# Splitting four of the stores by rows: the last one, and three of the side stores, in a decode layer with its backward pass

## The chip, the cores and the metric

The kernel runs on one core of a Trainium2 chip. The core has TensorE (matmul and transpose), VectorE, ScalarE and GpSimd for computing, SyncE (SP), which here only issues transfers, and sixteen DMA engines that carry data between HBM and the on-chip memory (SBUF, 128 partitions). The metric is the device time of one execution in microseconds, lower is better.

## The reference, cut to what matters

One decode step (batch 4, one new token, width 512) of a pre-norm transformer layer with a cached attention (32 heads, 4096 cached positions, head size 128) and a gated feed-forward part of width 1792, forward and backward:

```python
def _A_ref(x, k_cache, v_cache, wq, wo):
    q = (x @ wq).reshape(B, Sq, H, Dh).transpose(0, 2, 1, 3)
    scores = jnp.einsum("bhqd,bhkd->bhqk", q, k_cache) * (Dh ** -0.5)
    p = _softmax(scores, axis=-1)
    o = jnp.einsum("bhqk,bhkd->bhqd", p, v_cache)
    return o.transpose(0, 2, 1, 3).reshape(B, Sq, H * Dh) @ wo
def _B_ref(x, w1, w3, w2):
    h = _silu(x @ w1) * (x @ w3)
    return h @ w2
h = x + _A_ref(_layernorm(x), k_cache, v_cache, wq, wo)
out = h + _B_ref(_layernorm(h), w1, w3, w2)
```

The outputs are `out` and its vector-Jacobian products with a given `grad_out`, in bfloat16: for x (`out_1`), for k_cache (`out_2`), for v_cache (`out_3`), for wq (`out_4`), wo (`out_5`), w1 (`out_6`), w3 (`out_7`) and w2 (`out_8`). There is one query position only, so the gradient of each of the 128 heads' K is the outer product of a column of 4096 numbers and a row of 128 (likewise for V). The two cache gradients are by far the largest outputs: 4 x 32 x 4096 x 128 numbers each, 134 MB. The gradient of each weight is an outer product too, summed over the 4 rows of the batch.

## The kernel before, in words

All large data lives in one SBUF tensor, `arena`, cut into 23 slots of 4160 numbers a partition (`Slot`). Two neighbouring slots together are a `Slot2`. A slot is taken from a list of free ones, filled, used, and given back; who takes it next waits for the transfer that last read or wrote it. The order of the work of every engine is the order of the program text: the schedule is manual.

Forward. Heads are read one after the other, K and V, a slot each (1024 KB: 128 partitions of 8 KB). VectorE and TensorE transpose K, TensorE makes the scores, and a small matrix is kept for each head for the gradient of q. Then comes the feed-forward part with its gradients for h.

Backward. V is read a second time. The first 32 heads are done one at a time (`front`, `group_dS`, `grad_K`, `grad_V`), the other 96 heads in 48 pairs: a pair fills a `Slot2`, 128 partitions of 16 KB, 2048 KB. In the loop over pairs (`for t in range(NT)`), in this order: V pairs are loaded ahead (`load_pairs`, L1319); `front_pair` transposes a pair of V (TensorE L795, ScalarE L796) and multiplies it with the incoming gradient (L1351); `more_V` makes pairs of the gradient of V (`grad_pair` to `out_3`); `grad_pair` to `out_2` makes the pair's gradient of K. `grad_pair` takes a `Slot2`, lets VectorE write the outer product (`outer_pair`, L1422) and stores it with one transfer on SP's queue (L1432). GpSimd prepares the columns for these products (`P2_pair`, L1419) and the windows for `front_pair` (`dO_pair`, L1331). The very last of these stores, that of `out_2` for pair 47, is the last transfer of the program.

Between these, `side(s)` advances the generator `side_work` by a step or two. It makes the small gradients: x and wq, then w2 (two stores of 128 rows of 7 KB, L1174), w1 and w3 (four stores, L1190), and wo (four stores of 128 rows of 8 KB, L1201). Each piece of 512 columns is one matmul (`grad_unit`), copied out of the accumulator by ScalarE (L1030) one piece later (`grad_flush`). When a slot is full, its store is issued on SP's queue, in 128 rows, one a partition.

All transfers but a few tiny ones go through SP's queue, in program order. SP uses eight semaphores for them in turn, so a transfer is issued only when the eighth before it has landed. GpSimd's own queue carries the few tiny ones (for instance the four rows of `oflat`, L1179).

Of the kernel before, what the change touches and what calls it, by code (L numbers as in the profile page):

```python
# [29 lines left out]
def kernel(  # L30
# [22 lines left out]
    nc = tc.nc  # L53
    P = nc.NUM_PARTITIONS

    B = A_x.shape[0]
    D = A_x.shape[-1]
    H = A_k_cache.shape[1]
    Sk = A_k_cache.shape[2]
    Dh = A_k_cache.shape[3]  # L60
# [6 lines left out]
    SJ = Sk // P  # L67
# [138 lines left out]
    for i in range(2):  # L206
        t = fcon.tile([P, 64], BF16, name=f"onesw{i}")
# [4 lines left out]
    def ones_window(col):  # L212
# [11 lines left out]
                          in_=rowg[:, None, :, None].to_broadcast([P, 4, 8, 4]))  # L224
# [635 lines left out]
    with ExitStack() as cm:  # L860
# [72 lines left out]
        for fc in range(FC):  # L933
            c = fc % 2
# [82 lines left out]
    with ExitStack() as c2:  # L1017
# [9 lines left out]
        def grad_flush():  # L1027
            if gu:
                dst, ps, n = gu.pop()
                nc.scalar.copy(out=dst, in_=ps[:, 0:n])  # L1030


        def grad_unit(dst, lhsT, rhs):
            n = rhs.shape[-1]
            ps = psg.tile([P, 512], FP32, tag="gps", name="gps")
            nc.tensor.matmul(ps[:, 0:n], lhsT=lhsT, rhs=rhs, start=True, stop=True)
            grad_flush()
            gu.append((dst, ps, n))
# [33 lines left out]
        def side_work():  # L1072
# [10 lines left out]
            t = rs.f(2048)[:, 1536:1536 + NH]  # L1083
# [49 lines left out]
            for cc in range(DC):  # L1133
                st = Slot("gwq")
# [32 lines left out]
            for i in range(2):  # L1167
                st = Slot("gw2")
                hw = hh_rows[:, i * 7 * P:(i + 1) * 7 * P].rearrange("b (p k) -> b k p", k=7)
                for k in range(7):  # L1170
                    grad_unit(st.b(7 * D)[:, k * D:(k + 1) * D], hw[:, k, :], gr_bf)
                    yield
                grad_flush()
                nc.sync.dma_start(out=out_8[i * 7 * P:(i + 1) * 7 * P, :].rearrange("(p c) j -> p c j", c=7),  # L1174
                                  in_=st.b(7 * D).rearrange("p (c j) -> p c j", c=7))
                st.give()
            oflat = Slot("oflat")
            for b in range(B):
# [1 line left out]
            for (rows, out_ap) in ((dg_rows, out_6), (du_rows, out_7)):  # L1180
                for i in range(2):
                    st = Slot("gw13")
                    nw = hhat_bf[0:B, i * 2 * P:(i + 1) * 2 * P].rearrange("b (p k) -> b k p", k=2)
                    for k in range(2):
                        for (f0_, w_) in f_chunks:
# [5 lines left out]
                                      in_=st.b(2 * F).rearrange("p (c f) -> p c f", c=2))  # L1191
                    st.give()
            r1.give()
            for h0 in range(0, H, 8):
                st = Slot("gwo")
                ow = oflat.b(HD)[0:B, h0 * P:(h0 + 8) * P].rearrange("b (p k) -> b k p", k=8)
                for k in range(8):
                    grad_unit(st.b(8 * D)[:, k * D:(k + 1) * D], ow[:, k, :], dh_bf)
                    yield
                grad_flush()  # L1200
                nc.sync.dma_start(out=out_5[h0 * P:(h0 + 8) * P, :].rearrange("(p k) j -> p k j", k=8),  # L1201
                                  in_=st.b(8 * D).rearrange("p (k j) -> p k j", k=8))
                st.give()
            oflat.give()
            r2.give()
            part["side_done"] = True

        units["s"] = side_work()


# [91 lines left out]
        NT = (NH - SP) // 2  # L1302
# [8 lines left out]
        def two_heads(ap, t):  # L1311
            b, h = t % B, H0 + t // B * 2
            return ap[b, h:h + 2].rearrange("h (p j) d -> (h p) (j d)", p=P // 2)
# [107 lines left out]
        def outer_pair(dst, col2, row):  # L1421
            nc.vector.tensor_tensor(  # L1422
                out=dst.rearrange("p (j r t) -> p j r t", r=Dh // 2, t=2),
                in0=col2[:, :, None, :].to_broadcast([P, 2 * SJ, Dh // 2, 2]),
                in1=row.rearrange("p (r t) -> p r t", t=2)[:, None, :, :].to_broadcast([P, 2 * SJ, Dh // 2, 2]),
                op=ALU.mult,
            )

        def grad_pair(out_ap, t, col2, row):
            g_ = Slot2()  # L1430
            outer_pair(g_.t[:, 0:2 * SJ * Dh], col2, row)
            nc.sync.dma_start(out=two_heads(out_ap, t), in_=g_.t[:, 0:2 * SJ * Dh])  # L1432
            g_.give()

        O0, S0, S1, L, LP = 2, 21, 35, 5, 3
# [2 lines left out]
        def more_V(upto):  # L1438
            while gvd["n"] < min(SP, upto):
                s = gvd["n"]  # L1440
                P_group(s // B)
                replicate("rdo", s - s % REP)
                grad_V(s)
                P_group(s // B + 1)
                gvd["n"] += 1
                if s % REP == 2 and 2 < s < SP - 2:
                    replicate("rdo", s + 2)
                elif s == SP - 2:
                    replicate_pair("rdo", 0)
                if s >= SP - 2:  # L1450
                    P2_pair(s - SP + 2)
            while gvd["t"] < NT and SP + 2 * gvd["t"] + 2 <= upto:
                t = gvd["t"]
                P2_pair(t)
                replicate_pair("rdo", t // B)
                grad_pair(out_3, t, pP2.pop(t), reps["rdo", "p", t // B][:, t % B, :])
                P2_pair(t + 1)
                gvd["t"] += 1
                if t % B == 2:
                    replicate_pair("rdo", t // B + 1)  # L1460
# [57 lines left out]
        for t in range(NT):  # L1518
            s = SP + 2 * t
            load_pairs(t + LP)  # L1520
            if t % B == 2:
                replicate_pair("rq", t // B + 1)
            if t + LP < NT:
                front_pair(t + LP, lambda: side(s))
            else:
                if t + LP == NT:
                    rows_out()
                    rows_T()
                side(s)
            more_V(s + 2 + lead_V(s))  # L1530
            grad_pair(out_2, t, pdS[t // 2][:, t % 2], reps["rq", "p", t // B][:, t % B, :])
            if t % 2 == 1 and t + 1 < NT:
                group_dS_pair((t + 1) // 2)
            side(s + 1)
# [31 lines left out]
```

## Time and profile before

| | |
|---|---|
| time, median of 3 runs | 1681.93 us (1681.45 to 1684.35) |
| the profiled execution's own time | 1680.53 us |
| its span, first to last instruction | 1678.7 us |
| moved by DMA | 705.31 MB, mean 420 GB/s |
| HBM read / written | 420.75 MB / 282.34 MB |
| TensorE / VectorE / ScalarE / GpSimd busy | 75% / 71% / 58% / 23% |
| a 2048 KB store, issue to landing (median) | 27.3 us |
| issue of an SP transfer (L1432, median) | 0.33 us |

Times in the views are microseconds from the start of the span. The page cuts the span into 40 equal slices; the digits after an engine's name are its busy share in tenths, those after DMA the mean busy share of the sixteen DMA engines. "Issue to landing" is the time until the last of the sixteen engines' shares has arrived; the trace records all sixteen landings of each transfer, but not by the engines' numbers. A window's line gives the stretch, its length, busy time and number of instructions of each computing engine, the granted TensorE clock, the DMA share and GB/s. DMA shares come from whole packets, so in short windows they are coarse, and a full load can read 1.01 or 1.02. A line of waits says who waited for whom: total us, times, longest.

### The profile page before, as it was taken

Reading aid. Unit: us, or ns where it says so; the run is one execution under the profiler, and the core shown is the slowest. Engines: PE = TensorE matmul, PEld = TensorE weight load, DVE = VectorE, ACT = ScalarE, POOL = GpSimd, SP = SyncE. Lnnn points to the kernel's source line nnn. Section 1 sums busy time; section 2 is a strip of 40 time slices with the busy share of each in tenths; the row PEclk is TensorE's granted clock in tenths of the full one; section 3 lists DMA queues with packets and bytes.
Section 4 is the critical chain, followed back from the end, with each engine's and each line's share of the span. In section 5 each row is a group of like instructions: output and inputs, shape, how many; then the busy total and the mean of one; then the engine's idle time right before and its main releaser. Section 6 shows DMA issues by size and latency. Waiting matters only on the chain.

```text
span 1678.7 us, 33156 instructions
## 1 busy us (share of the span) xinstructions
PE 1264.2 (75%) x13899; PEld 884.7 (53%) x13899; DVE 1194.9 (71%) x1000; ACT 969.8 (58%) x1545; POOL 381.1 (23%) x665
## 2 busy tenths in 40 slices
PE   5999889889888889877777657667667777767650
PEld 4777777777677776643433334444444444444330
DVE  5888888888888887667766558586566566555683
ACT  3555545555555554677667557567666676666650
POOL 1221223222232223333313313211111112101020
PEclk9999999999999999899999888886666676666775
DMA  9999999999999999999999999999999999999996
GB/s 402 419 425 424 425 425 425 425 423 424 415 417 407 424 403 411 405 407 426 426 427 428 429 430 430 430 430 429 430 430 430 429 429 432 429 431 430 429 430 285
DMA packets 82229, 705.31 MB, mean 420 GB/s; under 512 B 8716, under 2 KB 14744, under 8 KB 16544
## 3 DMA queue, kind: packets, MB, share of 16 engines
q1 hardware_dynamic: 81664, 703.10, 99.3%
q8 instruction: 109, 1.79, 0.4%
q14 instruction: 40, 0.33, 0.0%
q0 software_dynamic: 416, 0.10, 0.0%
HBM read 420.75 MB, written 282.34 MB: 419 GB/s over the span
## 4 chain that ended last, share of the span: by engine, by line
DMA 74%; DVE 10%; PE 8%; ACT 3%; issue 2%; DVEq 0%; POOL 0%; SPq 0%; ACTq 0%
DMA out_dram<-arena 38%; DMA arena<-in_A_k_cache_dram 27%; DMA arena<-in_A_v_cache_dram 7%; DVE arena L1422 7%; PE M_ps L468 2%; ACT arena L796 2%; PE pt_tps L355 1%; DVE arena L830 1%; DVE arena L454 1%; DMA arena<-arena 1%; ACT Pn L433 1%; DMA arena<-in_A_wq_dram 1%; PE pt_tps L795 1%; DMA arena<-in_A_wo_dram 1%; PE b_ps L411 1%
## 5 line engine op out<-in xcount | busy, mean ns | idle before, releaser
L796 ACT COPY arena<-pt_tps 128x1024 bf16<-128x1024 bf16 x512 | 491.1, 1026 | 243.7 <-PE pt_tps L795 240.4
L795 PE MATMUL pt_tps<-ident_f,arena 128*128 128x128 f32 x2048 | 400.7, 348 | 200.8 <-DMA arena<-in_A_v_cache_dram 116.2
L795 PEld LDWEIGHTS pt_tps<-ident_f,arena 128*128 128x128 f32 x2048 | 292.9, 176 | 371.0 <-issue 189.3
L1422 DVE TENSOR_TENSOR arena<-arena 128x8192 bf16<-128x8192 bf16 x48 | 212.4, 4426 | 203.4 <-DMA out_dram<-arena 183.8
L454 DVE TENSOR_TENSOR arena<-arena 128x4096 bf16<-128x4096 bf16 x128 | 289.9, 2265 | 4.9 <-POOL arena L450 4.6
L468 PE MATMUL M_ps<-arena 128*128 128x130 bf16 x4096 | 282.4, 221 | 4.5 <-DMA arena<-in_A_v_cache_dram 4.3
L468 PEld LDWEIGHTS <-arena 128*128 128x128 bf16 x4096 | 252.8, 99 | 20.9 <-DMA arena<-in_A_v_cache_dram 11.1
L1422 DVE TENSOR_TENSOR arena<-dS,arena 128x8192 bf16<-128x8192 bf16 x48 | 212.4, 4427 | 54.9 <-DMA out_dram<-arena 54.9
L361 DVE STREAM_TRANSPOSE arena<-arena 128x512 f32<-128x512 f32 (+1 forms) x258 | 239.9, 947 | 0.0
L356 ACT COPY arena<-pt_tps 128x1024 bf16<-128x1024 bf16 x128 | 127.8, 1013 | 183.8 <-PE pt_tps L355 183.5
L1419 POOL COPY arena<-arena 128x128 bf16<-128x128 bf16 x48 | 48.2, 1005 | 385.2 <-DVE arena L1422 266.7
L367 POOL TENSOR_TENSOR W<-qrep,wmask 128x128 bf16<-128x128 bf16 x128 | 113.9, 890 | 82.8 <-PE S_ps L387 68.2
L450 POOL COPY arena<-P_all 128x64 bf16<-128x64 bf16 x128 | 31.0, 242 | 402.9 <-ACT P_all L444 296.8
L1331 POOL COPY arena<-arena 64x4 bf16<-64x4 bf16 x96 | 80.9, 843 | 135.6 <-PE dP_ps L1351 114.2
L355 PE MATMUL pt_tps<-ident_b,arena 128*128 128x128 bf16 x1024 | 79.7, 224 | 37.8 <-DMA arena<-in_A_k_cache_dram 37.6
L830 DVE TENSOR_TENSOR arena<-dS,arena 128x4096 bf16<-128x4096 bf16 x32 | 73.5, 2299 | 36.4 <-DMA out_dram<-arena 35.9
L433 ACT ACTIVATE Pn<-E,rl 128x1024 bf16<-128x1024 f32 x64 | 73.5, 1149 | 36.4 <-DVE rl L430 36.1
L1351 PE MATMUL dP_ps<-arena 128*32 128x512 bf16 x768 | 85.2, 479 | 7.0 <-ACT arena L796 6.8
L355 PEld LDWEIGHTS <-arena 128*128 128x128 bf16 x1024 | 62.5, 100 | 48.0 <-DMA arena<-in_A_k_cache_dram 47.0
L387 PE MATMUL S_ps<-arena,W 128*32 128x256 bf16 x1536 | 81.3, 285 | 0.5 <-DVE arena L361 0.2
L444 ACT COPY P_all<-pt_P 32x64 bf16<-32x64 bf16 x256 | 51.9, 203 | 48.6 <-PE pt_P L440 46.4
L478 PE MATMUL kP_ps<-arena,onesw 128*32 128x512 bf16 x1024 | 79.2, 386 | 0.0
(257 smaller groups left out, 1363.9 us busy)
## 6 DMA issues: line engine op xcount, KB each, us to landing
out_dram<-arena SPq DMA_DIRECT2D x96, 2048.0 KB, 27.3
arena<-in_A_v_cache_dram SPq DMA_DIRECT2D x160, 1024.0 KB, 16.2
arena<-in_A_k_cache_dram SPq DMA_DIRECT2D x128, 1024.0 KB, 17.9
arena<-in_A_v_cache_dram SPq DMA_DIRECT2D x48, 2048.0 KB, 31.7
out_dram<-arena SPq DMA_DIRECT2D x72, 1024.0 KB, 19.9
arena<-in_A_wq_dram SPq DMA_DIRECT2D x8, 1024.0 KB, 17.0
arena<-in_B_w_dram SPq DMA_DIRECT2D x6, 896.0 KB, 11.8
out_dram<-arena SPq DMA_DIRECT2D x6, 896.0 KB, 26.1
```

Of the source, the lines that this page charges most:

```text
L355: nc.tensor.transpose(pt[:, i, :], Kn[:, c * GW + i, :], ident_b[:])
L356: nc.scalar.copy(out=KT[:, c * GW:(c + 1) * GW, :], in_=pt[:])
L361: nc.vector.transpose(out=KT[:, c * w_:(c + n) * w_], in_=Kn[:, c * w_:(c + n) * w_])
L367: nc.gpsimd.tensor_tensor(out=W[:, hl], in0=qrep[:, :, s:s + 1].to_broadcast([P, 4, 32]), in1=wmask[:, hl, None, :].to_broadcast([P, 4, 32 ...
L433: nc.scalar.activation(out=st["Pn"][:], in_=st["E"][:, :, None, :].to_broadcast([P, JQ, 4, 32]), func=AF.Copy, scale=rl[:])
L454: nc.vector.tensor_tensor(out=PK[:, :, 0:Dh].rearrange("p j (r t) -> p j r t", t=2), in0=Ks[s].heads().rearrange("p j (r t) -> p j r t", t=2),
L468: nc.tensor.matmul(hold["M"][:], lhsT=Vn[:, j, :], rhs=PK[:, j, :], start=(j == 0), stop=(j == SJ - 1))
L795: nc.tensor.transpose(ptw[:, jj, :], w[:, 4 * g + jj, :], ident_f[:])
L796: nc.scalar.copy(out=v.rearrange("p (j d) -> p j d", d=Dh)[:, g * GW:(g + 1) * GW, :], in_=pt[:])
L830: nc.vector.tensor_tensor(out=dst.rearrange("p j (r t) -> p j r t", t=2), in0=col2[:, :, None, :].to_broadcast([P, SJ, Dh // 2, 2]), in1=r ...
L1351: nc.tensor.matmul(rows["acc"][32 * c:32 * (c + 1), :], lhsT=zt[t % B][:, k, ZP - m:ZP - m + 32], rhs=words_of(v, 2 * c + u, k), start=(pl ...
L1422: nc.vector.tensor_tensor(out=dst.rearrange("p (j r t) -> p j r t", r=Dh // 2, t=2), in0=col2[:, :, None, :].to_broadcast([P, 2 * SJ, Dh / ...
```

## The change

Four stores are cut by rows (partitions); the bytes, the source and the destination stay the same.

- The last store of all (`out_2`, pair 47, 128 rows of 16 KB) becomes two transfers on SP's queue: first rows 92 to 127 (36 rows), then rows 0 to 91 (92 rows, which run on four DMA engines).
- The two stores of the gradient of w2 (`out_8`, 128 rows of 7 KB) become three transfers each on SP's queue: 112, 11 and 5 rows for the first, 112, 10 and 6 rows for the second.
- The first of the four stores of the gradient of wo (`out_5`, 128 rows of 8 KB) becomes 112 rows on SP's queue and two parts, of 7 and of 9 rows, on GpSimd's queue.

```diff
@@ side_work, gradient of w2 @@
-                nc.sync.dma_start(out=out_8[i * 7 * P:(i + 1) * 7 * P, :].rearrange("(p c) j -> p c j", c=7),
-                                  in_=st.b(7 * D).rearrange("p (c j) -> p c j", c=7))
+                cuts = ((0, 112), (112, 123), (123, P)) if i == 0 else ((0, 112), (112, 122), (122, P))
+                for (p0, p1) in cuts:
+                    nc.sync.dma_start(out=out_8[i * 7 * P:(i + 1) * 7 * P, :].rearrange("(p c) j -> p c j", c=7)[p0:p1],
+                                      in_=st.b(7 * D).rearrange("p (c j) -> p c j", c=7)[p0:p1])
                 st.give()
@@ side_work, gradient of wo @@
-                nc.sync.dma_start(out=out_5[h0 * P:(h0 + 8) * P, :].rearrange("(p k) j -> p k j", k=8),
-                                  in_=st.b(8 * D).rearrange("p (k j) -> p k j", k=8))
+                for (eng, p0, p1) in ((nc.sync, 0, 112), (nc.gpsimd, 112, 119), (nc.gpsimd, 119, P)) if h0 == 0 else ((nc.sync, 0, P),):
+                    eng.dma_start(out=out_5[h0 * P:(h0 + 8) * P, :].rearrange("(p k) j -> p k j", k=8)[p0:p1],
+                                  in_=st.b(8 * D).rearrange("p (k j) -> p k j", k=8)[p0:p1])
                 st.give()
@@ grad_pair @@
-            nc.sync.dma_start(out=two_heads(out_ap, t), in_=g_.t[:, 0:2 * SJ * Dh])
+            last = out_ap is out_2 and t == NT - 1
+            for (p0, p1) in ((92, P), (0, 92)) if last else ((0, P),):
+                nc.sync.dma_start(out=two_heads(out_ap, t)[p0:p1], in_=g_.t[p0:p1, 0:2 * SJ * Dh])
             g_.give()
```

The order of the computing engines' instructions stays as it was. SP issues five transfers more, GpSimd two.

## The prediction

> **What bounds the kernel now.** I read the page first, for what the whole span is limited by.
>
> ```profile
> span 1678.7 us, 33156 instructions
> DMA  9999999999999999999999999999999999999996
> GB/s 402 419 425 424 425 425 425 425 423 424 415 417 407 424 403 411 405 407 426 426 427 428 429 430 430 430 430 429 430 430 430 429 429 432 429 431 430 429 430 285
> q1 hardware_dynamic: 81664, 703.10, 99.3%
> DMA 74%; DVE 10%; PE 8%; ACT 3%; issue 2%; DVEq 0%; POOL 0%; SPq 0%; ACTq 0%
> ```
>
> All sixteen DMA engines are busy in every slice but the last, and from the middle on they move 430 GB/s without a dip. TensorE, VectorE and ScalarE have room. So no compute instruction is worth anything here, and only two things are: fewer bytes (the change moves the same bytes) and the way the engines finish. The last slice stands at six tenths. I therefore looked at the DMA view of the last 39 us alone, in slices of 0.975 us, and at windows over the same stretch (the last two columns are DMA share and GB/s).
>
> ```profile
> DMA  9897999989999899999997755520000000000000
> GB/s 437 370 504 336 504 437 387 487 370 471 437 387 504 353 471 437 387 504 387 437 420 303 336 235 252 235 118 34 34 17 34 17 34 34 17 34 17 34 0 0
> ```
> ```profile
> 1650.00:1660.00 10.00, 0.00 (x0) 0.00 (x0) 1.85 (x1) 0.00 (x0) 0.00 (x0) 0.50 1.02 437
> 1664.00:1665.00 1.00, 0.00 (x0) 0.00 (x0) 0.00 (x0) 0.00 (x0) 0.00 (x0) 0.50 0.57 246
> 1667.00:1677.00 10.00, 0.00 (x0) 0.00 (x0) 0.00 (x0) 0.00 (x0) 0.00 (x0) 0.50 0.07 28
> ```
>
> Until 1660 the share is 1: sixteen engines. At 1664 it is 0.57, about nine. From 1667 to 1677 it is 0.07, and 1/16 is 0.0625: for ten microseconds one engine alone works off its part of the last stores at 28 GB/s, about what each of sixteen has at 430 GB/s (26.9). The kernel's end is this one engine. The trace's landing records, sixteen for each transfer, say it exactly. The last store's sixteen shares landed at 1660.74, then 1661.24, 1661.25, 1661.30 and 1661.43, then nothing until 1663.41 and 1663.88, then eight between 1665.51 and 1666.91, and the last at 1677.82; the span ends 0.9 later. The late engine is not an accident of the end: its landing behind the median one is 1.7 us for a store issued at 731, 3.8 at 913, 5.7 at 1095, 8.7 at 1299, 10.8 at 1483, 12.3 for the last.
>
> Third, the issue side, for what stands behind the last store.
>
> ```profile
> SPq L1432 <- DVE arena L1422: 567.7, 93, 13.8
> 1643.21 9.00 SPq L1432 DMA_DIRECT2D out_dram<-arena  x3
> DMA to landing us min/median/max: 15.4/27.3/31.8
> ```
>
> The last store is issued at 1651.88 and lands 25.9 us later, behind what its engines have queued. SP mostly waits for VectorE, so another issue of 0.33 us (median of that line) is hidden.
>
> **The change part by part.** The sum is made against the profiled execution: span 1678.7, own time 1680.53, so 1.83 outside the span. The median of the three runs, 1681.93, is 1.4 above it; I carry the difference over to the median.
>
> *A row.* A 2048 KB store is 128 rows of 16 KB, eight an engine. At 430 GB/s it takes 2.097 MB / 430 = 4.88 us, 0.61 us a row; the late engine's last landings are 4.83 to 4.87 apart, 0.607 a row, which I use. The tail shows that an engine working alone keeps that rate. Rows of 7 KB and 8 KB are taken in proportion, 0.267 and 0.305.
>
> *Last store.* Before, eight rows on each engine. After, 92 rows on four engines, 23 each, and 36 rows. That 92 go on four I read as the largest equal division over at most sixteen (92 = 4 x 23); then 36 go on twelve, 3 each, and I assume both counts start from the same end of the row of engines. The four then have 26 rows (18 more, +10.93 us), the next eight have 3 (5 fewer, -3.04), the remaining four none (8 fewer, -4.86). [...]
>
> *Side stores* (L1174 twice, L1201 once). By the same division 112 rows give 7 an engine, and 11 + 5 (then 10 + 6) put one row each on the first eleven and five (ten and six). The first four gain one row of 7 KB in each, +0.53; the last four lose one in each, -0.53. Of the out_5 store, 16 of 128 rows go as 7 + 9 through GpSimd: any engine loses one 8 KB row and gets zero to two, so -0.31 to +0.31; I take 0, as sixteen rows over sixteen engines.
>
> *Issues.* Five more on SP, each 0.33 us: hidden by the 567.7 us above. Two on GpSimd, 0.54 us each (median of the four at L1179), at about 1493 behind the wait for ScalarE; behind them stand GpSimd's L1331 and L1419 copies for the next pair, and VectorE's L1422 waits for the latter. GpSimd is 23% busy and sits idle 8 to 12 us before these copies at that place, and those VectorE products wait for slots anyhow (226 us). Nothing. Without the cover it would be 1.1 us.
>
> *A wait that is added.* SP's transfers use eight semaphores in turn, and each waits for the landing of the eighth before it. Four more issues near 1319 and 1341 shorten that reach: the load issued at 1319.47 would wait for the store issued at 1298.82, which landed at 1323.83, 4.4 us late; the next ones come some 3 to 7 us late. All transfers behind it in SP's order are late with it. It costs nothing as long as each engine still has work queued: the earliest share of that same store landed 13.1 us after its issue, and the late engine's 25. If the cover were gone, engines that are early now would lose up to 7 us, the late one none.
>
> *Sum, if the four engines are early ones and the late engine is among those that get nothing of the last store:* late engine 1677.82 - 4.86 - 0.53 = 1672.43; the four 1661.43 + 10.93 + 0.53 = 1672.89; middle ones below 1667. The last landing moves from 1677.82 to 1672.9, **4.9 us earlier**: span 1673.8, profiled time 1675.6, median **1677.0** (-0.29%).
>
> **Which engines are they?** The profile does not number them, and this is the weakest step. What it shows: the four that land within 0.19 us of each other have kept together, 3.6 to 3.8 us ahead of the median one, for stores issued from 1483 to 1606 as well. They are the one block of four that behaves alike, as neighbours with the same extra traffic would; the late engine is alone and in no block. [...]
>
> **The rivals.**
>
> 1. *The late engine is among the eight that get 3 rows.* It keeps them: 1677.82 - 3.04 = 1674.8, 3.0 earlier, 1678.9. For: eight places of sixteen. Against: nothing in a row. [...]
> 2. *The four are middle engines.* The latest of them decides: 1665.5 to 1666.9, plus 11.46, is 1677.0 to 1678.4, so 0.8 earlier to 0.6 later: 1681.1 to 1682.5. Here also belongs that the division does nothing (every engine still eight rows, 1681.9). [...]
> 3. *Slower: the late engine is one of the four.* It gets 18 more rows: 1677.82 + 11.46 = 1689.3, 11.5 later, 1693.4 (+0.68%). The point is 1677.82 - 11.46 = 1666.4: a block whose latest member now lands after that loses. Blind, that is 4 places in 16; the block above speaks against it.
> 4. *The semaphore wait empties the early engines,* by up to 7 us. With the forecast's places the four then end at up to 1679.9, 2.1 later, 1684.0. Against: 13 us of backlog.
>
> **How the numbers follow.** The forecast 0.62, rival 1 0.14, rival 2 0.12, rival 3 0.10, rival 4 0.02. Three runs spread over 2.9 us, so 0.2% (3.4 us) is about what can be told from no change. The forecast alone, with the 0.3 of the out_5 rows and 1 us of scatter, is 1675.7 to 1678.3, all of it faster by over 0.2%. Rival 1 at -3.0 lies just within, and I give a fifth of it, 0.03, to faster: faster 0.65; same 0.11 + 0.12 and half of rival 4 for 0.24; slower 0.11. The range goes from 1675.7 over rivals 1 and 2 to 1682.5 and leaves out rivals 3 and 4.
>
> **What would show it.** In the after trace: a last stretch at a DMA share of about 0.25 (four engines), from about 1667 to 1672, in place of ten microseconds at 0.07, and a span near 1674. A share of 0.07 to the end at about 1674.8 is rival 1; 0.25 up to 1678 is rival 2; one engine until 1689 is rival 3; a DMA share well under 1 between 1320 and 1360 is rival 4. Of the side stores I expect the parts of few rows to land before the 112-row part. The prediction is wrong if the late engine or the early block sits elsewhere in the row, or if four engines alone don't keep 0.607 us a row.

## The result, and the profile after

| | before | after |
|---|---|---|
| time, median of 14 runs each | 1682.03 us (1679.65 to 1684.35) | 1686.29 us (1683.67 to 1689.18) |
| the profiled execution's own time | 1680.53 us | 1683.67 us |
| its span | 1678.7 us | 1681.9 us |

The changed kernel is slower: ratio 1.0024, with a 95% interval of 1.0016 to 1.0033, so 4.3 us of 1682. The forecast was 4.9 us faster. The profiled execution of the changed kernel is the fastest of its 14 and lies 2.6 us below their median, that of the kernel before 1.5 us below its own, so the traces show 3.2 us of the 4.3.

The page of the changed kernel: the span, the sixteen DMA engines' busy share and rate in 40 slices of 42 us, and the chain that ended last by engine.

```profile
span 1681.9 us, 33168 instructions
DMA  9999999999999999999999999999999999999996
GB/s 401 419 425 424 425 425 425 426 423 424 413 420 404 425 402 412 407 407 427 426 427 428 429 431 429 430 430 429 430 430 430 422 416 431 429 425 419 429 431 290
DMA 73%; DVE 10%; PE 10%; ACT 3%; issue 2%; DVEq 0%; SPq 0%; POOL 0%; ACTq 0%
```

The busy digits are the same as before. What is new are two dips in a rate that stood at 429 to 431 before: 422 and 416 in the slices from 1304 to 1388 us, where the two `out_8` stores are cut, and 425 and 419 from 1472 to 1556, where the `out_5` store's rows pass. Windows over the two stretches (the last two columns are DMA share and GB/s), before and after:

```profile
1330.00:1370.00 40.00, 28.57 (x151) 17.57 (x144) 21.15 (x10) 26.57 (x36) 7.36 (x14) 0.70 1.01 428
1500.00:1530.00 30.00, 22.07 (x116) 13.26 (x116) 17.19 (x10) 20.99 (x27) 1.15 (x3) 0.72 1.00 428
```
```profile
1330.00:1370.00 40.00, 28.48 (x142) 17.36 (x138) 19.57 (x10) 25.78 (x35) 7.33 (x13) 0.66 1.01 408
1500.00:1530.00 30.00, 21.49 (x97) 13.73 (x96) 16.52 (x9) 19.09 (x25) 2.56 (x5) 0.63 1.01 409
```

The share stays at 1 and the rate falls by 20 GB/s. So the engines don't wait for an issue: they are busy and slower. The trace's packet records say how. A packet of 16 KB takes 0.611 us, one of 8 KB 0.309 and one of 7 KB 0.272. Between 1300 and 1400 us three packets of these sizes took over one and a half times that before, and 48 after; between 1490 and 1560 it was 3 and 36; behind 1650 it was none and 12. In the last group the twelve take 0.92 to 2.18 us, and five of them 1.27, about double; between 1300 and 1400 the 16 KB ones scatter around a median of 1.14. Below I call those that took over one and a half times their usual time *slow packets*.

The end of the span, 1640 to 1682, in slices of 1.05 us, with the issues of that stretch:

```profile
DMA  9998999999999989999988765342323322232100
GB/s 437 453 453 359 484 437 406 421 453 437 390 453 453 453 359 484 437 406 390 390 374 359 328 265 234 140 156 94 109 94 109 125 109 125 109 125 94 62 0 0
out_dram<-arena SPq DMA_DIRECT2D x3, 2048.0 KB, 28.6
out_dram<-arena SPq DMA_DIRECT2D x1, 1472.0 KB
out_dram<-arena SPq DMA_DIRECT2D x1, 576.0 KB
```

Before, one engine alone went on for ten microseconds at a share of 0.07. Now the tail stands at two or three tenths and mostly 94 to 125 GB/s until 1679: at 27 GB/s an engine that is the work of three and a half to four and a half. The landing records show which, by their numbers and times:

| store (last three transfers) | before | after |
|---|---|---|
| the store before the last: first landing, the 15th, the 16th | 1655.88, 1662.06, 1672.98 | 1657.94, 1667.46, 1678.89 |
| the 36 rows: landings, the last two | | 12, at 1669.28 and 1680.72 |
| the 92 rows: landings | | 4, at 1676.49, 1679.59, 1679.79, 1680.55 |
| the last store of 128 rows: the 15th, the 16th | 1666.91, 1677.82 | |

(A transfer of fewer than sixteen shares also shows one landing record within 1.2 us of its issue, which is left out of the counts.) The late engine finishes the store before the last at 1678.89, and 1.83 us later, three rows, it lands a share of the 36 rows. So it is among the twelve and not among the four. Of the four, with 26 rows each, three end within 1.2 us of it and one at 1676.49.

SP's issues around the first cut store, as the timeline of the changed kernel shows them (start, duration, engine, line):

```profile
1318.97 1.17 SPq L1176 DMA_DIRECT2D out_dram<-arena  x3
1323.85 0.37 SPq L1322 DMA_DIRECT2D arena<-in_A_v_cache_dram  x1
1328.81 0.36 SPq L1437 DMA_DIRECT2D out_dram<-arena  x1
1333.60 0.34 SPq L1322 DMA_DIRECT2D arena<-in_A_v_cache_dram  x1
1340.78 6.14 SPq L1176 DMA_DIRECT2D out_dram<-arena  x3
```

And its largest group of waits (us in all, times, longest):

```profile
SPq L1437 <- DVE arena L1425: 542.1, 89, 13.9
```

The load that was issued at 1319.47 goes out at 1323.85: the prediction's added wait, to 0.02 us. The second cut store's three issues take 6.14 us: the second goes out at 1343.73 and the third at 1346.65, right behind the landings of the eighth transfer before each, at 1343.72 and 1346.63. SP still mostly waits for VectorE.

**The late engine's account.** Its landings, compared with those of the kernel before for the same transfers, in the profiled executions: no later until 1344; 1.65 us later after the two `out_8` stores; 2.8 after the `out_5` store; steady until 1658. Its shares of the last two full stores then take 6.57 and 6.28 us (landings 1666.04, 1672.61, 1678.89) in place of 4.85 each: 3.1 more. Five rows fewer in the last store save 3.0. 2.8 + 3.1 - 3.0 = +2.9, and 1677.82 + 2.9 = 1680.7: that is where it lands, and the end of the span.

So two losses have to be explained, 2.8 us in the side stores and 3.1 in the tail. The experiments go by four theories. S: what costs is which rows an engine is sent to: while a transfer of other than 128 rows passes, some packets take about twice their time (1.27 us in place of 0.611 in the tail above). P: only the number of rows of each engine counts. W: the added semaphore waits. U: the unequal number of rows. Of the `out_5` store also G: GpSimd's queue.

### The profile page after: what moved, and what is told of

It reads as the page before. It is cut to its first block, busy times and chain, and to the rows that moved or that the text cites. A ratio compares the mean times of both kernels' runs of the same rounds, so it can differ in the third digit from the quotient of the medians.

```text
span 1681.9 us, 33168 instructions
## 1 busy us (share of the span) xinstructions
PE 1267.0 (75%) x13899; PEld 886.2 (53%) x13899; DVE 1195.1 (71%) x1000; ACT 970.3 (58%) x1545; POOL 388.2 (23%) x667
## 4 chain that ended last, share of the span: by engine, by line
DMA 73%; DVE 10%; PE 10%; ACT 3%; issue 2%; DVEq 0%; SPq 0%; POOL 0%; ACTq 0%
DMA out_dram<-arena 44%; DMA arena<-in_A_k_cache_dram 26%; DVE arena L1425 7%; PE M_ps L468 3%; DMA arena<-in_A_v_cache_dram 2%; PE pt_tps L355 1%; DVE arena L830 1%; ACT Pn L433 1%; ACT arena L796 1%; DVE arena L454 1%; PE b_ps L411 1%; ACT E L419 1%; PE S_ps L387 1%; PE pt_P L440 1%; DMA arena<-in_A_wq_dram 1%
## 5 line engine op out<-in xcount | busy, mean ns | idle before, releaser
L1334 POOL COPY arena<-arena 64x4 bf16<-64x4 bf16 x96 | 91.3, 951 | 101.3 <-PE dP_ps L1354 92.1
```

The costliest lines, as they stand in the source:

```text
L1334: nc.gpsimd.tensor_copy(out=zt[t % B][r_, :, ZP + 2 * i:ZP + 2 * i + 2], in_=zt[B][r_, :, s - SP:s2 - SP + 1:B])
```

## The experiments

Each run was taken in five rounds beside the kernel before; ratios are to that kernel's runs on the same chip. The median of before is 1681.79 us beside the first four and 1682.37 beside the last four. All eight kernels do the whole computation.

### The last store alone

The last part of the change, without the others:

```diff
-            nc.sync.dma_start(out=two_heads(out_ap, t), in_=g_.t[:, 0:2 * SJ * Dh])
+            last = out_ap is out_2 and t == NT - 1
+            for (p0, p1) in ((92, P), (0, 92)) if last else ((0, P),):
+                nc.sync.dma_start(out=two_heads(out_ap, t)[p0:p1], in_=g_.t[p0:p1, 0:2 * SJ * Dh])
```

> Only the last store is cut (36 + 92 rows); all side stores as before. [...] Rival P (places alone: the late engine carries 3 of the 36 rows, the four have 26 rows, all rows at 0.61 us): -3.0 us, no slow packets. Rival W (the waits for the eighth transfer before are what costs): -3.0 us too, since here no side store is cut.

Measured: 1682.46 us, ratio 1.0005 (0.9996 to 1.0014), span 1678.7, as before. The tail of its trace (1640 to 1682, DMA share and rate):

```profile
DMA  9998999999999989788764233233222211000000
GB/s 453 406 468 374 484 406 437 421 421 453 421 453 406 468 375 453 328 374 328 281 218 187 125 156 140 94 140 125 94 125 109 94 62 47 16 16 0 0 0 0
```

The four engines (100 to 140 GB/s) are done by 1676.3, and what ends last is one engine alone (16 GB/s in these coarse slices). It has three rows in place of eight here, and lands at 1677.81; before it was 1677.82. Its landings stand 7.3 and 5.5 us apart for the last two full stores where 4.85 each was its rate: 3.1 us lost against 3.0 saved. There are 13 slow packets behind 1650. S holds; P and W, which had 3.0 us of gain here, fall.

### The `out_8` stores alone

```diff
-                nc.sync.dma_start(out=out_8[...].rearrange("(p c) j -> p c j", c=7),
-                                  in_=st.b(7 * D).rearrange("p (c j) -> p c j", c=7))
+                cuts = ((0, 112), (112, 123), (123, P)) if i == 0 else ((0, 112), (112, 122), (122, P))
+                for (p0, p1) in cuts:
+                    nc.sync.dma_start(out=out_8[...].rearrange("(p c) j -> p c j", c=7)[p0:p1],
+                                      in_=st.b(7 * D).rearrange("p (c j) -> p c j", c=7)[p0:p1])
```

> Only the two gradient-of-w2 stores are cut (112 + 11 + 5, 112 + 10 + 6 rows). Theory S: the last engine comes 1.6 us later by 1380, as in the changed kernel's trace, and keeps this to the end: +1.6 us, between +1.0 and +2.5; GB/s falls to about 390 to 415 between 1340 and 1370. Rival P: the late engine is one of the first five and gets one 7 KB row more in each store, +0.53 us, nothing else. Rival W: the same +1.6 as S, but then it must also show when the store is cut by columns.

Measured: 1684.40 us, ratio 1.0015 (1.0007 to 1.0024), span 1682.6. Its windows over the two stretches:

```profile
1330.00:1370.00 40.00, 27.07 (x149) 15.93 (x147) 19.08 (x9) 25.80 (x34) 8.46 (x15) 0.71 1.01 410
1500.00:1530.00 30.00, 22.10 (x119) 13.18 (x122) 17.73 (x9) 21.49 (x28) 2.07 (x2) 0.73 1.01 430
```

The dip is where the cut is, and only there: 410 against 428, and 430 in the other stretch. There are 47 slow packets between 1300 and 1400, and the late engine falls back by 2.4 us across the cut. The ratio stands for 2.5 us, at the upper end of what S had forecast and far above P's 0.5; W is not yet told from S here.

### The `out_5` store alone

```diff
-                nc.sync.dma_start(out=out_5[...].rearrange("(p k) j -> p k j", k=8),
-                                  in_=st.b(8 * D).rearrange("p (k j) -> p k j", k=8))
+                for (eng, p0, p1) in ((nc.sync, 0, 112), (nc.gpsimd, 112, 119), (nc.gpsimd, 119, P)) if h0 == 0 else ((nc.sync, 0, P),):
+                    eng.dma_start(out=out_5[...].rearrange("(p k) j -> p k j", k=8)[p0:p1],
+                                  in_=st.b(8 * D).rearrange("p (k j) -> p k j", k=8)[p0:p1])
```

> Only the first gradient-of-wo store is cut (112 rows on SP, 7 + 9 on GpSimd). Theory S: +1.2 us, between +0.5 and +2.5, with GB/s at about 400 to 415 between 1500 and 1530. Rival P: between -0.3 and +0.3. Rival W: 0, since SP issues no transfer more.

Measured: 1683.04 us, ratio 1.0009 (1.0000 to 1.0018), span 1682.8. Its windows:

```profile
1330.00:1370.00 40.00, 29.55 (x151) 17.64 (x150) 19.78 (x10) 26.26 (x35) 8.46 (x15) 0.63 1.01 430
1500.00:1530.00 30.00, 21.29 (x110) 13.37 (x106) 16.08 (x9) 19.98 (x26) 3.37 (x5) 0.67 1.00 408
```

Again the dip goes with the cut, 408 against 428, with 39 slow packets between 1490 and 1560; the late engine falls back by 1.6 us. The three parts add up: +0.7, +2.6 and +1.3 us of medians make +4.5 against the +4.3 of the whole change.

### The same issues and waits, cut by columns

This takes the cut of rows away and keeps everything else of the `out_8` part: three transfers for each of the two stores, at the same places in SP's order, with 128 rows in each.

```diff
-                nc.sync.dma_start(out=out_8[...].rearrange("(p c) j -> p c j", c=7),
-                                  in_=st.b(7 * D).rearrange("p (c j) -> p c j", c=7))
+                for (c0, c1) in ((0, 5), (5, 6), (6, 7)):
+                    nc.sync.dma_start(out=out_8[...].rearrange("(p c) j -> p c j", c=7)[:, c0:c1],
+                                      in_=st.b(7 * D).rearrange("p (c j) -> p c j", c=7)[:, c0:c1])
```

> [...] SP's issues and their waits for the eighth transfer before are those of the change. Theory S: no slow packets, 430 GB/s through 1340 to 1370, 0 us against before, -0.5 to +0.7 (the 1 KB rows cost some 0.3 us). Rival W (waits): +1.6 us as with the cut by rows. Rival P: 0.

Measured: 1682.34 us, ratio 1.0002 (0.9993 to 1.0011), span 1678.7. Its windows:

```profile
1330.00:1370.00 40.00, 28.62 (x143) 17.76 (x142) 21.54 (x10) 26.37 (x36) 6.83 (x12) 0.70 1.01 425
1500.00:1530.00 30.00, 22.45 (x116) 13.49 (x116) 17.22 (x9) 21.09 (x27) 1.27 (x2) 0.72 1.01 430
```

SP's issues around the first of these stores, as the timeline of this run shows them:

```profile
1318.45 1.37 SPq L1175 DMA_DIRECT2D out_dram<-arena  x3
1323.31 0.34 SPq L1320 DMA_DIRECT2D arena<-in_A_v_cache_dram  x1
1338.31 6.88 SPq L1175 DMA_DIRECT2D out_dram<-arena  x3
```

425 GB/s (S had said 430; before it was 428), 7 slow packets, and a late engine that is 0.35 us later across the cut, against 2.4 with the cut by rows. The load that waited until 1323.85 waits here until 1323.31. So the wait is there and costs nothing that can be measured. The interval of the ratio reaches up to 1.9 us and alone would not exclude W's 1.6; the late engine's 0.35 does: W falls, and four transfers more cost no more than that either. What costs is the cut by rows.

### Even halves

Two transfers of 64 rows in place of 112 + 11 + 5. Every engine carries the same number of rows, four and four (the page counts 81696 packets on SP's queue, 32 more than before, so each half has sixteen shares):

```diff
+                for (p0, p1) in ((0, 64), (64, P)):
+                    nc.sync.dma_start(out=out_8[...].rearrange("(p c) j -> p c j", c=7)[p0:p1],
+                                      in_=st.b(7 * D).rearrange("p (c j) -> p c j", c=7)[p0:p1])
```

> [...] Rival U (it is the unequal number of rows that puts the engines out of step): no slow packets beyond the 3 of before, 0 us.

Measured: 1684.29 us, ratio 1.0013 (1.0004 to 1.0022), span 1681.4. The window over the cut:

```profile
1330.00:1370.00 40.00, 26.99 (x151) 15.64 (x147) 19.57 (x10) 27.33 (x36) 8.09 (x15) 0.72 1.01 410
```

410 GB/s and 48 slow packets, as with the uneven cut; the late engine falls back by 1.6 us. The number of rows that each engine carries is not the cause: U falls. What is left is which rows an engine is sent to.

### The last store as 60 + 68 rows

If S is right, it matters which rows the four engines get. Here they are given the upper ones, 17 each; the late engine gets four of the 60 lower ones in place of eight.

```diff
-            nc.sync.dma_start(out=two_heads(out_ap, t), in_=g_.t[:, 0:2 * SJ * Dh])
+            last = out_ap is out_2 and t == NT - 1
+            for (p0, p1) in ((0, 60), (60, P)) if last else ((0, P),):
+                nc.sync.dma_start(out=two_heads(out_ap, t)[p0:p1], in_=g_.t[p0:p1, 0:2 * SJ * Dh])
```

> Only the last store is cut: rows 0-59 (fifteen engines, 4 rows each), then rows 60-127 (four engines, 17 each). Rival P (places alone): the late engine 4 rows fewer, 1677.8 - 2.4 = 1675.4; the four 13 rows more, at most 1674.8: -2.4 us, no slow packets. [...]

Measured: 1679.08 us (1677.28 to 1682.05), ratio 0.9983 (0.9974 to 0.9992), span 1677.1: faster than the kernel before and than the changed one. The tail (1640 to 1682):

```profile
DMA  9999999999999998997797733223211000000000
GB/s 390 468 421 421 406 499 406 421 421 468 421 390 468 437 421 375 468 359 312 328 406 312 296 140 156 125 125 140 109 47 47 31 31 16 0 0 0 0 0 0
```

Four engines at 110 to 155 GB/s until 1670, then ever fewer, and one alone at the last, done at 1676. The late engine's last full store and its four rows land at 1673.79 and 1676.21, 2.42 us apart: four rows at its own rate. There are 4 slow packets behind 1650. The four engines end at 1669.9 to 1672.6. The medians' gain of 3.3 us (1.3 to 4.4 by the ratio) is above the 2.4 that P allowed; the late engine's gain in the trace is the 2.4 of four rows, so this run alone doesn't tell P from S.

### The same numbers of rows, the other way up

The four engines get the lower 68 rows, 0 to 67, and the late engine's share comes from the upper 60. Every engine carries as many rows as in the run above (81667 packets on SP's queue in both), in the same order of issue.

```diff
+            for (p0, p1) in ((68, P), (0, 68)) if last else ((0, P),):
```

> Only the last store is cut, with the same numbers of rows for each engine as in the cut 60 + 68: rows 68-127 (fifteen engines, 4 each), then rows 0-67 (four engines, 17 each). Rival P: the same as there, -2.4 us. [...]

Measured: 1681.13 us, ratio 0.9993 (0.9985 to 1.0002), span 1678.1. The tail (1640 to 1682):

```profile
DMA  9999999999999999898877334223332000000000
GB/s 390 468 453 406 406 484 406 406 437 484 406 390 468 453 390 359 343 343 281 296 281 281 140 140 156 109 125 125 109 78 62 16 16 31 16 0 0 0 0 0
```

The four end at 1670.9 to 1674.6, and while they read, the late engine is held up: its last full share takes 7.3 us (1667.4 to 1674.7) where 4.85 was its rate, and it ends alone at 1677.19. There are 30 slow packets behind 1650, against 4. The medians of the two runs stand 2.05 us apart, with nothing but the rows exchanged. The intervals of the two ratios overlap a little (0.9985 to 0.9992), but of the 121 pairs of one execution from each run, 101 have the one with the lower 68 rows slower. The late engine loses 2.4 us here and had 2.4 to gain. The last landings of the two traces are only 0.98 us apart, as the two profiled executions differ before the cut already: the late engine lands the store issued at 1632.17 here at 1657.71, the same store of the run above at 1659.24. From there on this run loses 2.5 us.

### The `out_5` store on SP's queue alone

112 and 16 rows, both on SP's queue, none on GpSimd's:

```diff
+                for (p0, p1) in ((0, 112), (112, P)) if h0 == 0 else ((0, P),):
+                    nc.sync.dma_start(out=out_5[...].rearrange("(p k) j -> p k j", k=8)[p0:p1],
+                                      in_=st.b(8 * D).rearrange("p (k j) -> p k j", k=8)[p0:p1])
```

> Only the first gradient-of-wo store is cut, 112 + 16 rows, both on SP's queue; nothing on GpSimd. Every engine still carries eight rows (7 + 1). Theory S: slow packets between 1490 and 1560 as with the 7 + 9 on GpSimd (39 there), +0.5 to +2.5 us. Rival G (GpSimd's queue is the cause): none, 0 us.

Measured: 1682.62 us, ratio 0.9999 (0.9990 to 1.0007), span 1680.0. The window over the cut:

```profile
1500.00:1530.00 30.00, 23.61 (x113) 14.23 (x113) 16.13 (x9) 19.52 (x24) 0.14 (x1) 0.60 1.01 414
```

414 GB/s and 26 slow packets without any transfer on GpSimd's queue: the packets are slow because of the cut and not because of the queue, so G falls as the cause of them. The time is another matter. The late engine is 1.1 us later across this cut in its trace, but the ratio shows no loss, and S had forecast 0.5 to 2.5 us: its point missed, though the interval (up to 1.2 us) leaves it possible. Against the 1.3 us of the cut with GpSimd the intervals overlap, so how much of that belongs to GpSimd's queue stays open.

## Why the prediction was wrong, point by point

- **What bounds the kernel** (sixteen full engines and one late one at the end): right. The late engine lands last in every run whose tail is shown, and its landings account for the end.
- **Rows divided by counts:** right. The landings are 12 for 36 rows, 4 for 92, and 11, 5, 10 and 6 for the small parts.
- **The late engine among those that get no row of the last store, -4.86:** wrong. If all parts are counted from the same engine, which the trace doesn't show, it is the fifth in SP's order: it has a share in the parts of 5, 6, 10, 11 and 36 rows (landings at 1347.19, 1364.38, 1364.10, 1346.91 and 1680.72, each 6.6 to 11.4 us behind the next latest) and none in the 92. So it keeps three rows and saves 3.0: rival 1's place.
- **The side stores' -0.53 for it:** wrong in sign, by the same mistake. As the fifth it has a row of each small part, so +0.53 by rows alone. Of the 2.8 us that it lost there, 0.5 are those rows, and the other 2.3 are put down to the slow packets. The parts of few rows also landed after the 112-row part (1346.91 and 1347.19 against 1346.63) and not before it, as the prediction had expected.
- **The four as the early block, 1672.9:** wrong. Worked back from their landings by 23 rows of 0.607 us, if they kept that rate, three of them ended their part of the 36 rows at 1665.6, 1665.8 and 1666.6, in the middle of the twelve (1659.8 to 1669.3, and the late one), so they are middle engines, as in rival 2; the fourth, by the same working, ended it at 1662.5 or before. Three of them reach 1679.6 to 1680.6, level with the late engine. No run shows whether a transfer on four engines takes neighbours, since the trace doesn't number the engines; that it takes the four that land alike was the author's guess, and the four here land between 1676.49 and 1680.55.
- **0.607 us a row, whoever reads it:** this step turned the sign. The prediction had no rival for it, and named it as a doubt only for the four. It was the engine beside them that didn't: 6.57 and 6.28 us for eight rows in place of 4.85, while the 92 rows were read. By places alone, and with the 0.5 of the side stores' rows, the late engine would have come 2.5 earlier, at 1675.3; the four ended at 1676.3 in the run of the last store alone, so the kernel would still have gained some 1 to 1.5. The missing terms of the late engine are +3.1 in the tail (the last store alone: nothing gained) and +2.3 in the side stores.
- **The added wait, at nothing:** right in its place (1323.85 against 1323.83) and its price (cut by columns: 1.0002); the DMA share stays at 1.01 between 1330 and 1370, so rival 4 did not come about. **The issues on SP, at nothing:** right by the same run. **Sixteen rows through GpSimd, at 0 with ends of 0.31:** the store's cut measured +1.3 us, with an interval from 0 to 3; which part is GpSimd's was not settled.
- **The rival on the slower side** (the late engine one of the four, 1693.4): not what happened. The kernel is slower for another reason and by less.

What the rows have to do with it is shown by the runs of 60 and 68 rows: the same shares for each engine, other rows, 2.05 us. Whether it is the SBUF side or the HBM side that makes the packets slow is not shown, since each row is at once an SBUF partition and a stretch of HBM. One thing in the trace speaks for the SBUF side: of the 48 slow packets between 1300 and 1400, 41 are of 16 KB, so they belong to loads and stores of other HBM tensors than the one whose store was cut. No run here moved the SBUF rows apart from the HBM rows, and which rows the late engine carries in a store of 128 is not shown either.

A store cut in two by rows was not without effect: by the medians the even halves lost 1.9 us, and the run of 60 and 68 rows gained 3.3.

Two things stay open besides: why this one engine falls behind by some 1.2% from 720 us on (in the kernel before, 1.7 us behind the median engine for the store issued at 731 and 12.3 for the one at 1597; in the changed one 1.1 at 731 and 11.8 at 1600); and why the `out_8` cut sets the late engine back by 2.4 us alone and by 1.65 within the whole change. Single executions of one kernel scatter by 5 us, and the account by landings is one of single executions.

## What to carry to other kernels

While all DMA engines are busy, cut a store by columns rather than by rows, if it has to be cut: here three transfers of all 128 partitions cost nothing that could be measured, while a cut by rows cost up to 2.6 us for stores that were hidden otherwise. Read the end of a DMA-bound kernel by each engine's last landings and not by the share of busy time; if one engine alone is late, fewer rows for it can be worth their time, but which rows the engines that take them over get counts too: by the medians, four engines on rows 60 to 127 gained 3.3 us here, on rows 0 to 67 1.2, on rows 0 to 91 nothing. A busy share of 1 with a falling rate (428 to 408 GB/s) was the sign of it here.

## What the runs showed that was not expected

- While a cut by rows passes, single packets of 16 KB take around 1.1 us, and up to 2.2, in place of 0.61. S's doubling, 1.27, is met by five of the twelve in the changed kernel's tail; the others scatter. The busy share hides this; the rate shows it (428 to 408 GB/s).
- A cut by rows of a store in mid-kernel, 350 us ahead of the end, is still there at the end: with the two `out_8` stores cut alone, the late engine's 2.4 us stay to its last landing, since it has no slack to lose, whatever the other fifteen have.
- Even halves cost about as much as 112 + 11 + 5 (ratios of 1.0013 and 1.0015), while three transfers by columns cost nothing that could be measured (1.0002).
- Which 68 rows the four engines took was worth 2.05 us, and with the better choice the last store's split gained 3.3 us by the medians, 0.17% by the ratio (0.08 to 0.26).
